# Unused matmuls, transposes and a value step moved in the opening; three second-layer groups first in each new chunk

## The chip, the cores and the metric

The kernel runs on one core of one Trainium2 chip. The core has five engines that run side by side and wait for each other through semaphores: the tensor engine (PE, with the loading of its weights shown apart as PEld), the vector engine (DVE), the scalar engine (ACT), the GpSimd engine (POOL) and the sync engine (SP). Transfers are issued from the queues of SP, ACT and POOL.

The metric is device time in microseconds (us). Before the change the median of 4 runs is 345.02 us (344.25 to 345.93). The execution that was profiled took 344.6 us, of which 342.9 us are the span from the first to the last instruction.

## The reference

Eight batches of eight-head causal attention over 576 tokens, with 16 "beacon" keys and values ahead that every query sees, then two dense layers with a leaky ReLU between:

```python
scores = scale * np.matmul(q, k_all.transpose(0, 1, 3, 2))   # q 8x8x576x64, k_all 8x8x592x64
scores = np.where(causal, -1000000000.0, scores)
...
a = np.exp(scores)
a /= a.sum(-1, keepdims=True) + 1e-09
attn_out = np.matmul(a, v_all)
...
x = attn_out.transpose(0, 2, 1, 3).reshape(4608, 512)
h = x @ w_in                    # 512 -> 2048
g = np.maximum(0.01 * h, h)
out = g @ w_out                 # 2048 -> 512
```

## The kernel before

**Attention.** The 64 heads are taken two at a time: a pair g (0 to 31, four to a batch) has one head in partitions 0 to 63 and the other in 64 to 127. For a pair the kernel turns q and k so that the head dimension lies on partitions, multiplies keys by queries into a score tile in PSUM, takes the exponential on ACT (line 262, or 310 for later pairs), clears what lies above the diagonal on POOL (line 275), multiplies by the values together with a column of ones (line 342, "value"), and divides on DVE (lines 351 and 352). The result x_nat is turned into xT, 512 features by 4608 tokens.

Pairs 0 to 7 (the opening, two batches) are turned on PE: `t_q` (line 217) issues 18 small transposes for q or k of a pair (line 229), and DVE or ACT copies the result out of PSUM (line 235). Pairs 8 to 31 are turned by DMA from SP (line 165), and so is their x_nat (lines 376 to 384).

**The dense layers.** Tokens are taken in nine chunks of 512. For a chunk, `up` (line 467) is one of 16 first-layer groups: four matmuls of 512 columns (line 395) and a leaky ReLU on ACT into gT (line 402). `down` (line 474) is one of 16 second-layer groups: four matmuls (line 433); four such groups make one 128-row output tile, which DVE copies to osb (line 445) and SP sends out (line 446). A chunk's second layer needs all of its first layer.

**Order.** The order of every engine's instructions is the order in which the program issues them. In the opening it is written out by hand as strings of steps: `q3` and `k3` are the transposes of pair 3 with their copies, `s2.1` is score tile 1 of pair 2 with its exponential, `m2.1` is a part of its masks on POOL, `v0.0` is the first half of the value product of pair 0, `l5.0` is a load of q (5.1: of k) for pair 5, `V` loads values, `i` and `o` load halves of the two weights, `x` turns a pair's x_nat on PE, `u` and `d` are one `up` and one `down`. `w6` is six unused matmuls of a zero matrix with 128 columns (line 480), and `W0.0.4` four of 112 columns that go into the PSUM buffer that `v0.0` will use (line 485). They compute nothing that is read.

From pair 8 on a list of events (lines 597 to 619) says at which point in the sequence of pairs loads, turns, score blocks, value steps and x turns are issued, and ahead of each event the program issues so many `up` and `down` groups through `fill` (line 456) that the rest is spread evenly. The plan keeps back KEPT = 3 groups for the moment when a new chunk of tokens becomes ready (`finish`, line 503, at the last pair of a batch). At that moment `finish` sets `turn` to 1, and `fill` then alternates: a `down`, an `up`, a `down`, and so on while second-layer groups are left.

```python
        if can1 and (turn[0] == 0 or not can2):
            up()
        elif can2:
            down()
```

The first `up` of a new chunk reads the xT that the last pair's x turn writes by DMA.

Of the kernel before, what the change touches and what calls it, by code (L numbers as in the profile page):

```python
# [15 lines left out]
def kernel(  # L16
# [93 lines left out]
    def make_ones():  # L110
        for t in v_bufs:
            nc.vector.memset(t[:, :, :, D : D + 1], 1.0)
# [30 lines left out]
    def load_qk(g, which):  # L143
        b, hp, grp, rows = where(g)
        loaded["qk", g, which] = nc.gpsimd.dma_start(  # L145
            out=raw_of(b, grp)[which][rows],
            in_=(q, k)[which][b, 2 * hp : 2 * hp + 2].rearrange("h (p i) d -> p h i d", i=RI),
        )
# [119 lines left out]
    def mask(g, part):  # L268
        aT = probs[g]
        for lo, n, rows in MASKS[part]:  # L270
            triangle(aT, lo, n, rows)
# [87 lines left out]
    def x_transposes(g, copy):  # L359
        b, hp = divmod(g, NPAIR)  # L360
        x_nat, _ = xs.pop(g)
        ps = ps_one.tile([128, 1024], BF16, name="tp", tag="one")
        for t, (q0, rows) in enumerate(QT):
            nc.tensor.transpose(
                ps[:, q0 : q0 + rows],
                x_nat[0:rows, t].rearrange("p e d -> p (e d)"),
                ident[0:rows, 0:rows],
            )
        copy(out=xT[:, hp, b * S : (b + 1) * S], in_=ps[:, 0:S])
# [81 lines left out]
        nc.scalar.copy(out=osb[:, n:], in_=acc[:, n:])  # L451
        nc.scalar.dma_start(out=out[t0 : t0 + 128, n:], in_=osb[:, n:])

    done1, done2, ready, turn, first_down = [0], [0], [0], [0], [0]

    def fill():
        i1, fc = divmod(done1[0], NF)
        i2, n2 = divmod(done2[0], NF)
        can1 = i1 < ready[0] and (i1 < 2 or i2 > i1 - 2)
        can2 = i2 < NCH and i2 < i1 and done1[0] >= first_down[0]  # L460
        if can1 and (turn[0] == 0 or not can2):
            up()
        elif can2:
            down()
        return can1 or can2

    def up():
        i1, fc = divmod(done1[0], NF)
        assert i1 < ready[0]
        moe1(i1, fc)  # L470
        done1[0] += 1
        turn[0] = 1

    def down():
        i2, n2 = divmod(done2[0], NF)
        moe2(i2, n2 // 4, n2 % 4)
        done2[0] += 1
        turn[0] = 0

    def unused(n, cols=128):  # L480
        ps = ps_one.tile([128, 512], FP32, name="av", tag="one")
        for i in range(n):
            nc.tensor.matmul(out=ps[:, 0:cols], lhsT=blank, rhs=blank[:, 0:cols], start=True, stop=True)  # L483
# [7 lines left out]
            )  # L491

    NG = B * NPAIR

    def has(g):
        return 0 <= g < NG

    dve, act, pool = nc.vector.tensor_copy, nc.scalar.copy, nc.gpsimd.tensor_copy

    def chunks_with(g):  # L500
        return (g + 1) // NPAIR * S // 512

    def finish(g, eng=0):
        if eng < 2 and g in xs:
            x_transposes(g, (dve, act)[eng])
        ready[0] = chunks_with(g)
        if g % NPAIR == NPAIR - 1:
            turn[0] = 1

    def run(steps):  # L510
        for step in steps.split():
            op, a = step[0], [int(x) for x in step[1:].split(".")] if step[1:] else []
            if op == "s":
                score(*a)
            elif op == "m":
                mask(*a)
            elif op == "v":
                value(*a)
            elif op == "x":
                finish(*a)  # L520
            elif op == "l":
                load_qk(*a)
            elif op == "V":
                load_v_cast(*a)
            elif op == "N":
                load_natural(*a)
            elif op == "T":
                turn_pair(a[0])
            elif op == "y":
                x_turn(a[0])  # L530
            elif op == "q" or op == "k":
                t_q(a[0], 0 if op == "q" else 1, (dve, act)[a[1] if len(a) > 1 else 0])
            elif op == "b":
                beacon_columns(a[0], (dve, act, pool)[a[1]])
            elif op == "u":
                up()
            elif op == "P":
                moe1_early(*a)
            elif op == "d":
                down()  # L540
            elif op == "w":
                unused(*a)
            elif op == "W":
                unused_ahead(*a)
            elif op == "i":
                load_w_in(a[0])
            elif op == "o":
                load_w_out(a[0])
            else:
                raise ValueError(step)  # L550
# [11 lines left out]
    with order:  # L562
        load_first_keys()
        load_beacon_k(0, 2, nc.scalar)
        nc.vector.memset(blank, 0.0)  # L565
        run("l0.0 l1.0")
        make_identity(nc, ident)
        make_ones()
        run("l1.1 l2.0 l2.1 V0.0 V0.1 V0.2 l3.0 l3.1 V0.3 V0.4 l4.0 l4.1 i0")
        make_pads()  # L570
        unused(24)
        cast_beacon_k(0, 2, nc.scalar.copy)
        beacon_transposes(0, 2)
        unused(10)
        nc.scalar.copy(out=k_nat0[:, :, 0], in_=first_k[:, 0])
        nc.vector.tensor_copy(out=k_nat0[:, :, 1], in_=first_k[:, 1])
        run("q0.1 k0 w6 s0.0 m0.0 q1 s0.1 k1 w6 s0.2 m0.1 w6 s0.3 m0.2")
        run("w6 s1.0 m1.0 q2 s1.1 k2 w6 s1.2 m1.1 w6 s1.3 m1.2 W0.0.4 s2.0 m2.0 W0.0.4 s2.1 v0.0 q3 l5.0 l5.1 s2.2 k3 m2.1 s2.3 i1 m2.2 W0.1.4 s3.0 m3.0 v1.0 s3.1 v0.1 s3.2 v1.1 m3.1 l6.0 l6.1 s3.3 x0.1 m3.2")
        run("v2.0 l7.0 l7.1 q4 v2.1 V1.0 V1.1 x1 k4.1 v3.0 v3.1 x2.1 s4.0 s4.1 x3 m4.0 V1.2 V1.3 V1.4 u s4.2 u s4.3 m4.1 m4.2 o0 u q5 k5 u")
        load_beacon_k(2, B, nc.gpsimd)  # L580
        run("s5.0 s5.1 m5.0 u u s5.2 s5.3 m5.1 m5.2 o1 u q6 k6 u v4.0 u v4.1 s6.0 s6.1 m6.0 u y4 N8.0 N8.1 u s6.2 s6.3 m6.1 m6.2 u")
        cast_beacon_k(2, B, nc.gpsimd.tensor_copy)
        run("q7 u k7 u v5.0 u v5.1 y5 N9.0 s7.0 s7.1 m7.0 d v6.0 v6.1 d y6 T8 s7.2 s7.3 m7.1 m7.2 N9.1 T9")
        beacon_transposes(2, B)
        run("b8.2 b9.2 b10.2 b11.2 u v7.0 v7.1 d d d d N10.0 N10.1 V2.0 V2.1 V2.2 V2.3 V2.4 d d N11.0 N11.1 x7")


        CUTS = [(0, 512, 1024, 1536, 1664), (0, 384, 896, 1376, 1664), (0, 224, 736, 1248, 1664)]
        BLOCKS = [((0, 0),), ((0, 1),)], [((0, 2),), ((0, 3), (1, 0))], [((1, 1),), ((1, 2),)], [((1, 3), (2, 0)), ((2, 1),)], [((2, 2),), ((2, 3),)]
        FIRST = 2 * NPAIR  # L590

        def block(g0, i):
            for tile in BLOCKS[i]:
                stretch([(g0 + r, CUTS[r][n], CUTS[r][n + 1]) for r, n in tile])

        events = []
        for g in range(FIRST, NG):
            if g > FIRST + 3:
                events.append((g - 3.6, 0, run, ("N%d.0" % g,)))
                events.append((g - 3.1, 0, run, ("N%d.1" % g,)))  # L600
            if g > FIRST + 1:
                events.append((g - 2.0, 0, run, ("T%d" % g,)))
            if g > FIRST + 3:
                events.append((g - 1.9, 0, run, ("b%d.2" % g,)))
            events.append((g + 2.25, 3, value, (g, 0)))
            events.append((g + 2.62, 4, value, (g, 1)))
            events.append((g + 2.63, 5, x_turn, (g,)))
            if (g - FIRST) % 3 == 0:
                for i in range(5):
                    events.append((g + (0.31 if g == FIRST else 0.01) + 0.6 * i, 2, block, (g, i)))  # L610
        ends = [FIRST]
        for g in range(FIRST, NG):
            events.append((g + 3.5, 2, finish, (g, 2)))
            if g % NPAIR == NPAIR - 1:
                ends.append(g + 3.5)
        for b in range(3, B):
            for n in range(NKB):
                events.append((4 * b - 0.9 + 0.3 * n, 6, load_v_cast, (b, n)))
        events.sort(key=lambda e: e[:2])
        KEPT = 3  # L620
        first_down[0] = 4
        w, d0 = 0, done1[0] + done2[0]
        for at, _, what, args in events:
            while w + 2 < len(ends) and at > ends[w + 1]:
                w, d0 = w + 1, done1[0] + done2[0]
            todo = 2 * NF * ready[0] - KEPT - d0
            aim = d0 + todo * (at - ends[w]) / (ends[w + 1] - ends[w])
            while done1[0] + done2[0] < aim and fill():
                pass
            what(*args)  # L630
        while done2[0] < NCH * NF:
            fill()
# [30 lines left out]
```

## Time and profile before

| what | us |
|---|---|
| median of 4 runs | 345.02 (344.25 to 345.93) |
| profiled execution | 344.6 |
| its span | 342.9 |
| ACT busy | 187.0 (55% of the span) |
| POOL busy | 181.1 (53%) |
| DVE busy | 81.6 (24%) |
| first-layer matmuls, 576 of 379 ns each on average | 139.0 |
| second-layer matmuls, 576 of 379 ns | 136.6 |
| value matmuls, 960 of 196 ns | 41.6 |
| score matmuls of pairs 8 to 31 | 24.4 |
| unused matmuls of 128 columns, 70 | 6.8 |

Matmuls are pipelined, so the duration of one matmul is longer than the distance from its start to the next one's; distances between starts are what a chain of them costs. A line of the timeline has the start, the time from first start to last end, the engine, the line of the kernel, what it writes and reads, the count, and in brackets the idle time ahead of it with what ended that. The profiler's clock row gives the share of the tensor engine's full clock that was granted.

### The profile page before, as it was taken

The page shows a single profiled execution, that of the slowest core. Times are in us where ns is not written, and L with a number is a line of the kernel's source. Part 1 is how long each engine was busy: PE and PEld are TensorE (multiplying, and loading weights), DVE is VectorE, ACT ScalarE, POOL GpSimd, SP SyncE. Part 2 cuts the span into 40 slices and gives each one's busy share as a digit, 9 for nine tenths or more (in the row PEclk, how much of TensorE's full clock was granted, in tenths as well). Part 3 has the DMA queues.
Part 4 walks back from the last instruction along what each step waited for, and adds up shares of the span by engine and source line. Part 5 has one row for each costly group of instructions (what it writes and reads, how often), then busy time and mean ns, then how long its engine had stood idle before and what let it go on. Part 6 is the DMA issues. An engine that isn't in the chain of part 4 may idle for free.

```text
span 342.9 us, 7415 instructions
## 1 busy us (share of the span) xinstructions
PE 333.1 (97%) x2978; PEld 168.6 (49%) x2978; DVE 81.6 (24%) x199; ACT 187.0 (55%) x280; POOL 181.1 (53%) x355
## 2 busy tenths in 40 slices
PE   8899999989998999999999999999999999999995
PEld 6574555435544454554454544554445544444442
DVE  4363343102322212221231123212321220000111
ACT  5868862668645784388347852775447205633300
POOL 8895878859998594488566965682211000000000
PEclk9989999999999999999999999999999999999999
DMA  9999999999999999999999999998211030000021
GB/s 140 132 204 178 142 194 152 186 126 169 157 159 175 169 140 120 142 125 135 131 153 112 137 125 132 132 135 97 81 54 45 19 109 32 0 31 32 31 92 61
DMA packets 154322, 40.16 MB, mean 117 GB/s; under 512 B 144384, under 2 KB 148608, under 8 KB 154288
## 3 DMA queue, kind: packets, MB, share of 16 engines
q0 software_dynamic: 100848, 18.54, 80.8%
q1 hardware_dynamic: 53024, 20.96, 33.3%
q8 instruction: 23, 0.38, 0.5%
q10 hardware_dynamic: 416, 0.20, 0.2%
q14 instruction: 11, 0.09, 0.1%
HBM read 37.22 MB, written 9.44 MB: 136 GB/s over the span
## 4 chain that ended last, share of the span: by engine, by line
PE 84%; DMA 8%; POOL 4%; DVE 1%; SPq 1%; issue 1%; ACT 0%; DVEq 0%; POOLq 0%
PE acc L395 35%; PE acc L433 32%; PE av L342 9%; PE sc L297 5%; DMA v_aug<-in_v_dram 5%; DMA xT<-x_nat 2%; DMA q_nat<-in_q_dram 2%; PE sc L253 2%; POOL v_aug L200 1%; POOL k_nat L157 1%; PE tp L229 1%; SPq L165 1%; POOL q_raw L145 0%; DVE qT L235 0%; POOL q_nat L157 0%
## 5 line engine op out<-in xcount | busy, mean ns | idle before, releaser
L395 PE MATMUL acc<-xT,w_in_sb 128*128 128x512 bf16 x576 | 139.0, 379 | 1.4 <-DMA xT<-x_nat 1.4
L433 PE MATMUL acc<-w_out_sb,gT 128*128 128x512 bf16 x576 | 136.6, 379 | 0.0
L402 ACT ACTIVATE gT<-acc 128x512 bf16<-128x512 f32 x144 | 85.2, 606 | 79.7 <-PE acc L395 79.0
L310 ACT ACTIVATE aT<-sc 128x1024 bf16<-128x1024 f32 (+3 forms) x96 | 76.8, 867 | 47.9 <-PE sc L297 46.3
L275 POOL TENSOR_SCALAR_AFFINE_SELECT aT<-aT 128x256 bf16<-128x256 bf16 (+2 forms) x160 | 57.6, 387 | 65.6 <-ACT aT L310 60.2
L433 PEld LDWEIGHTS <-gT 128*128 128x128 bf16 x576 | 53.7, 98 | 62.3 <-issue 2.5
L395 PEld LDWEIGHTS <-w_in_sb 128*128 128x128 bf16 x576 | 52.2, 98 | 60.5 <-issue 2.7
L445 DVE COPY osb<-acc 128x512 f32<-128x512 f32 x35 | 24.2, 691 | 92.1 <-PE acc L433 91.4
L351 DVE RECIPROCAL rec<-av 128x6 f32<-128x6 f32 (+1 forms) x64 | 12.0, 188 | 141.2 <-PE av L342 141.2
L342 PEld LDWEIGHTS <-aT 128*128 128x128 bf16 (+1 forms) x960 | 37.4, 99 | 15.2 <-issue 3.5
L342 PE MATMUL av<-v_aug,aT 128*128 128x65 bf16 (+1 forms) x960 | 41.6, 196 | 1.3 <-POOL aT L275 0.5
L157 POOL DMA_DIRECT2D k_nat<-in_k_dram x48 | 34.8, 731 | 4.0 <-DMA v_aug<-in_v_dram 3.0
L157 POOL DMA_DIRECT2D q_nat<-in_q_dram x48 | 34.8, 730 | 3.1 <-DMA v_aug<-in_v_dram 1.8
L200 POOL DMA_DIRECT2D v_aug<-in_v_dram x40 | 34.0, 857 | 3.2 <-DMA w_in_sb<-in_moe_w_in_dram 3.1
L352 DVE TENSOR_TENSOR x_nat<-av,rec 128x384 bf16<-128x384 f32 (+1 forms) x64 | 31.4, 490 | 2.2
L262 ACT ACTIVATE aT<-sc 128x1024 bf16<-128x1024 f32 (+3 forms) x32 | 26.5, 877 | 5.7 <-PE sc L253 5.6
L297 PE MATMUL sc<-qT,kT 64*128 64x208 bf16 (+16 forms) x368 | 24.4, 255 | 0.8 <-DMA kT<-k_nat 0.8
L297 PEld LDWEIGHTS <-kT 64*128 64x128 bf16 x368 | 12.3, 94 | 19.7 <-issue 17.9
L253 PE MATMUL sc<-qT,kT 64*128 64x80 bf16 (+4 forms) x96 | 10.4, 293 | 0.7 <-DVE kT L235 0.7
L235 DVE COPY qT<-tp 128x576 bf16<-128x576 bf16 x7 | 5.3, 754 | 13.3 <-PE tp L229 9.9
L483 PE MATMUL av<-blank 128*128 128x128 bf16 x70 | 6.8, 260 | 1.1 <-DVE blank L565 1.1
L451 ACT COPY osb<-acc 128x256 f32<-128x256 f32 x1 | 0.4, 372 | 13.7 <-DVE osb L449 13.7
(44 smaller groups left out, 67.4 us busy)
## 6 DMA issues: line engine op xcount, KB each, us to landing
out_dram<-osb SPq DMA_DIRECT2D x35, 256.0 KB, 2.6
q_nat<-in_q_dram POOLq DMA_DIRECT2D x48, 72.0 KB, 4.6
k_nat<-in_k_dram POOLq DMA_DIRECT2D x48, 72.0 KB, 4.7
v_aug<-in_v_dram POOLq DMA_DIRECT2D x24, 128.0 KB, 6.2
w_in_sb<-in_moe_w_in_dram POOLq DMA_DIRECT2D x2, 1024.0 KB, 12.0
w_out_sb<-in_moe_w_out_dram POOLq DMA_DIRECT2D x2, 1024.0 KB, 11.5
q_raw<-in_q_dram POOLq DMA_DIRECT2D x8, 144.0 KB, 8.1
k_raw<-in_k_dram POOLq DMA_DIRECT2D x7, 144.0 KB, 8.5
```

The costliest lines, as they stand in the source:

```text
L157: nc.gpsimd.dma_start(out=t[:, :, par], in_=(q, k)[which][b, 2 * hp + par].rearrange("(t p) d -> p t d", p=NR),)
L200: nc.gpsimd.dma_start(out=dst[lo : ROWS[c], c, :, 0:D], in_=v[b, :, OFF[c] : OFF[c] + n].rearrange("h p d -> p h d"),)
L262: nc.scalar.activation(out=aT[:, :, c0 : c0 + w], in_=sc[:, :, 0:w], func=AF.Exp, scale=0.125)
L275: nc.gpsimd.affine_select(out=view, in_=view, compare_op=ALU.is_ge, fill=0.0, base=128 - n if lo == 0 else 0, channel_multiplier=-1, patte ...
L297: nc.tensor.matmul(out=sc[:, par, at : at + b - a], lhsT=kT[ps_, c * 128 : (c + 1) * 128], rhs=qT[ps_, q0 : q0 + b - a], start=True, stop= ...
L310: nc.scalar.activation(out=probs[g][:, :, lo:hi], in_=sc[:, :, at : at + hi - lo], func=AF.Exp, scale=0.125)
L342: nc.tensor.matmul(out=avv[:, n, 0 : D + 1], lhsT=aT[0 : ROWS[c], par, a0 : a0 + 128], rhs=va[0 : ROWS[c], c, 2 * hp + par, :], start=(c = ...
L352: nc.vector.tensor_tensor(out=x_nat[:, t0:t1].rearrange("p t e d -> p (t e) d"), in0=avv[:, :, 0:D], in1=rec[:, n0:n1, None].to_broadcast( ...
L395: nc.tensor.matmul(out=acc, lhsT=w_in_sb[:, j, fc * 128 : (fc + 1) * 128], rhs=xT[:, j, i * 512 : (i + 1) * 512], start=(j == 0), stop=(j ...
L402: nc.scalar.activation(out=gT[i][:, fc, :], in_=acc, func=AF.Prelu, alpha=0.01)
L433: nc.tensor.matmul(out=acc, lhsT=gT[i][:, fc, t * 128 : (t + 1) * 128], rhs=w_out_sb[:, fc, :], start=(fc == 0), stop=(fc == NF - 1),)
L445: nc.vector.tensor_copy(out=osb, in_=acc)
```

## The change

1. The unused matmuls ahead of the beacon keys' transposes become 25 instead of 24, those behind them (ahead of pair 0's transposes) 13 instead of 10.
2. Pair 1's query transposes go behind score tile 0.1 instead of ahead of it, its key transposes behind tile 0.2 instead of 0.1; of the unused groups among pair 0's tiles, 6 + 6 become 5 + 4.
3. `v0.0` goes from ahead of `q3` to behind `k3`, and two more unused matmuls of 112 columns stand ahead of `s2.2`.
4. `q5` and `k5` go ahead: `q5` ahead of `s4.3`, `k5` ahead of an `up` and `o0`.
5. When a new chunk becomes ready, up to three second-layer groups are issued ahead of its first `up`, in place of the alternation from the first on.

```diff
-    done1, done2, ready, turn, first_down = [0], [0], [0], [0], [0]
+    done1, done2, ready, turn, first_down, held = [0], [0], [0], [0], [0], [0]
...
-        if can1 and (turn[0] == 0 or not can2):
+        if held[0] and can2:
+            held[0] -= 1
+            down()
+        elif can1 and (turn[0] == 0 or not can2):
             up()
...
+    KEPT = 3
...
         if g % NPAIR == NPAIR - 1:
             turn[0] = 1
+            held[0] = KEPT
...
-        unused(24)
+        unused(25)
         cast_beacon_k(0, 2, nc.scalar.copy)
         beacon_transposes(0, 2)
-        unused(10)
+        unused(13)
...
-        run("q0.1 k0 w6 s0.0 m0.0 q1 s0.1 k1 w6 s0.2 m0.1 w6 s0.3 m0.2")
-        run("... s2.0 m2.0 W0.0.4 s2.1 v0.0 q3 l5.0 l5.1 s2.2 k3 m2.1 s2.3 ...")
-        run("... u s4.2 u s4.3 m4.1 m4.2 o0 u q5 k5 u")
+        run("q0.1 k0 w6 s0.0 m0.0 w5 s0.1 q1 s0.2 m0.1 k1 w4 s0.3 m0.2")
+        run("... s2.0 m2.0 W0.0.4 s2.1 q3 l5.0 l5.1 W0.0.2 s2.2 k3 v0.0 m2.1 s2.3 ...")
+        run("... u s4.2 u q5 s4.3 m4.1 m4.2 k5 u o0 u")
...
-        KEPT = 3
```

In the strings "..." stands for steps that are the same in both. PE gets three matmuls more in all (4 + 2 added, 3 taken away). POOL's instructions keep their order.

More of the change, by code (lines that the diff above doesn't have):

```diff
@@ L570 @@
         make_pads()
-        unused(24)
+        unused(25)
         cast_beacon_k(0, 2, nc.scalar.copy)
         beacon_transposes(0, 2)
-        unused(10)
+        unused(13)
         nc.scalar.copy(out=k_nat0[:, :, 0], in_=first_k[:, 0])
         nc.vector.tensor_copy(out=k_nat0[:, :, 1], in_=first_k[:, 1])
-        run("q0.1 k0 w6 s0.0 m0.0 q1 s0.1 k1 w6 s0.2 m0.1 w6 s0.3 m0.2")
-        run("w6 s1.0 m1.0 q2 s1.1 k2 w6 s1.2 m1.1 w6 s1.3 m1.2 W0.0.4 s2.0 m2.0 W0.0.4 s2.1 v0.0 q3 l5.0 l5.1 s2.2 k3 m2.1 s2.3 i1 m2.2 W0.1.4 s3.0 m3.0 v1.0 s3.1 v0.1 s3.2 v1.1 m3.1 l6.0 l6.1 s3.3 x0.1 m3.2")
-        run("v2.0 l7.0 l7.1 q4 v2.1 V1.0 V1.1 x1 k4.1 v3.0 v3.1 x2.1 s4.0 s4.1 x3 m4.0 V1.2 V1.3 V1.4 u s4.2 u s4.3 m4.1 m4.2 o0 u q5 k5 u")
+        run("q0.1 k0 w6 s0.0 m0.0 w5 s0.1 q1 s0.2 m0.1 k1 w4 s0.3 m0.2")
+        run("w6 s1.0 m1.0 q2 s1.1 k2 w6 s1.2 m1.1 w6 s1.3 m1.2 W0.0.4 s2.0 m2.0 W0.0.4 s2.1 q3 l5.0 l5.1 W0.0.2 s2.2 k3 v0.0 m2.1 s2.3 i1 m2.2 W0.1.4 s3.0 m3.0 v1.0 s3.1 v0.1 s3.2 v1.1 m3.1 l6.0 l6.1 s3.3 x0.1 m3.2")
+        run("v2.0 l7.0 l7.1 q4 v2.1 V1.0 V1.1 x1 k4.1 v3.0 v3.1 x2.1 s4.0 s4.1 x3 m4.0 V1.2 V1.3 V1.4 u s4.2 u q5 s4.3 m4.1 m4.2 k5 u o0 u")
         load_beacon_k(2, B, nc.gpsimd)
```

## The prediction

> **What bounds the kernel now.** I read the page first, then the PE's list of waits, the granted clock by stage, and the timeline around each wait.
>
> ```profile
> PE 333.1 (97%) x2978; PEld 168.6 (49%) x2978; DVE 81.6 (24%) x199; ACT 187.0 (55%) x280; POOL 181.1 (53%) x355
> ```
>
> PE is busy for 97% of the span and no other engine for more than 55%. So PE sets the end, and this change hardly alters its work (three unused matmuls more). It can gain only idle time of PE and stretches in which PE ran at a lower clock. The list of PE's waits (us in total, times, longest) shows all idle time but the start and the end:
>
> ```profile
> PE acc L395 <- DMA xT<-x_nat: 1.4, 1, 1.4
> ...
> PE sc L297 <- DMA kT<-k_nat: 0.8, 1, 0.8
> PE sc L253 <- DVE kT L235: 0.7, 2, 0.4
> PE av L342 <- POOL aT L275: 0.5, 1, 0.5
> ```
>
> The clock, in a table by stage (stretch and its length; busy us and instructions of PE, PEld, DVE, ACT, POOL; granted clock; DMA). Column PEclk is the one to read:
>
> ```profile
> 11.57:14.99 3.42, 2.83 (x35) 1.52 (x32) 0.68 (x1) 3.42 (x5) 2.12 (x5) 1.00 2.95 127
> 14.99:18.40 3.41, 2.69 (x60) 1.75 (x61) 2.08 (x4) 1.83 (x3) 3.41 (x10) 1.00 1.65 150
> 18.40:21.81 3.41, 3.41 (x50) 2.50 (x49) 1.36 (x4) 2.46 (x3) 3.40 (x9) 0.50 1.13 208
> ```
>
> From 18.40 to 21.81 us PE ran at half clock, after a stretch in which it was busy 2.69 of 3.41 us. That loss is in no list of waits.
>
> **The change part by part.**
>
> *Extra unused matmuls (25 and 13).* The first group runs at 107 ns from start to start, so one more moves the beacon transposes from 3.74 to 3.85. The second group ran from 4.09 to 5.12 and PE then waited until 5.48 for pair 0's q, which landed at 5.4 (issued 1.33, 4.1 us to landing). Thirteen from 4.20 on (seven of about 107 ns, the rest at 56) have started by 5.2. Cost 0; if the clock rises later than at 4.75, all at 107 ns, they end near 5.6: 0.1 us.
>
> *Pair 1's transposes one tile later.* ACT works without a gap from 7.12 to 15.41 on the first ten score tiles. Now 0.1 starts at 7.3, ahead of ACT's need at 8.1; then q1 (0.40 us), 0.2 at 8.2 when its PSUM tile is free (8.56 before), k1 at 8.5; DVE has copied it by 9.7, ahead of 1.0 at 9.96. Cost 0 as long as that margin of 0.25 us lasts.
>
> *v0.0 behind k3.* This is the heart of the opening. Before:
>
> ```profile
> 13.76 0.37 PE L253 MATMUL sc<-qT,kT 64*128 64x464 bf16 x2
> 14.64 0.69 PE L342 MATMUL av<-v_aug,aT 128*128 128x65 bf16 x8 [0.51 <-POOL aT L275]
> 15.55 0.28 PE L342 MATMUL av<-v_aug,aT 128*128 128x65 bf16 x4 [0.23 <-DMA v_aug<-in_v_dram]
> 15.93 0.47 PE L229 MATMUL tp<-ident,q_raw 64*64 64x64 bf16 x18
> 16.33 0.35 PE L253 MATMUL sc<-qT,kT 64*128 64x336 bf16 x4
> 16.65 0.47 PE L229 MATMUL tp<-ident,k_raw 64*64 64x64 bf16 x18
> 17.05 0.30 PE L253 MATMUL sc<-qT,kT 64*128 64x208 bf16 x4
> 17.28 0.37 PE L489 MATMUL av<-blank 128*128 128x112 bf16 x4
> 18.05 0.39 PE L253 MATMUL sc<-qT,kT 64*128 64x512 bf16 x2 [0.39 <-DVE kT L235]
> ```
>
> It looks as if v0.0 held q3 up. But PEld shows that q3's first weight load also waited 0.22 us for its own data: pair 3's q was issued at 8.04 with 7.8 us to landing, so it is there at 15.84; its k (8.63 + 8.0) at 16.6. POOL's order is the same, so these landings stay. q3, now directly behind tile 2.1, stands idle from 14.1 to about 15.9, and behind it on PE wait tiles 2.2, 2.3, k3 and v0.0; ACT waits for 2.2 as before. Then: q3 15.93, two unused 16.33, tile 2.2 16.44 (16.33 before), k3 16.75, v0.0 17.15 (12 matmuls at 33 ns, 0.40), tile 2.3 17.55, four unused 17.8, tile 3.0 when DVE has copied k3. DVE takes q3 and k3 now without v0.0's division between, and ends at 17.98 (18.00 before). So tile 3.0 starts at 18.0 against 18.05: v0.0 fills the 0.39 us in which PE waited for that copy, and what was saved there is spent waiting at q3. v0.0's own division, now at 18.0, is needed only by x0. Bounds: were pair 3's data there in time, tile 2.2 would start near 14.7 and up to 1.3 us (ACT's gap there) would go; were the copies late, 0.4 lost. I take 0, by the landing.
>
> *The clock.* First the row: the loss of 18.40 to 21.81 is measured by the same chains at full clock elsewhere. There 12 value matmuls, a tile, 18, a tile, 18 took 0.78 + 0.50 + 1.10 + 0.46 + 0.92 = 3.76 us in the chain of waits; at full clock they take 0.37 + 0.30 + 0.66 + 0.28 + 0.66 = 2.27. Loss 1.5 us. The Trainium skill, "TensorE: Matmul & The Clock Gate" (HAM oscillation and the table behind it), asks only that PE have no idle gap over some 3 us; by that rule neither kernel would ever fall to half clock here and fillers are worth 0. The trace disagrees: the longest gap in the stretch was 0.51 us. [...]I sum, over each of the two stretches, columns streamed (0.44 us per 1000 columns, from 56 ns for 128, pairs on separate rows once): 50% from 11.57 to 14.99, no fall after it; 47% from 14.99, fall. With the new order I get some 47% and 52%: the first now has half of the idle time. (The page calls these stretches free-running; where they lie in other executions this trace does not show.) The same page's Part 4 says that transposes do not count as other matmuls do; without q3 and k3 the two become 47% and 38%, against 50% kept and 33% lost before. By the one count the fall may come at 15.0, by the other at 15.0 or 18.4; hardly any count removes it. Falling at 15.0 it would stretch q3 to tile 3.0: two transposes +0.2 each, tiles +0.3, v0.0 +0.3, unused +0.15, about 1.2 us for the 1.5. Bounds: -1.5 (no fall) to +1.2 (both). I take 0.
>
> *q5 and k5 earlier.* Tile 5.0 waited 0.34 us at 32.5 for k5's copy, with one `up` between. Now two `up` (1.7 us) stand between k5 and tile 5.0 and DVE is idle from 27.6: the wait goes, -0.34. q5's data landed at 26.3 and 27.0. o0's issue on POOL does not move.
>
> *Three second-layer groups first.* Timeline of the new chunk that waited:
>
> ```profile
> 106.44 0.81 PE L395 MATMUL acc<-xT,w_in_sb 128*128 128x512 bf16 x3
> 108.68 0.39 PE L395 MATMUL acc<-xT,w_in_sb 128*128 128x512 bf16 x1 [1.43 <-DMA xT<-x_nat]
> ```
>
> Three matmuls of `up` ran, the fourth waited 1.43 us for pair 11's xT: SP issued its last turn at 101.91 and it landed 6.7 us later. In the order of the new kernel two more `down` stand ahead of this `up`, 2 x 0.865 = 1.73 us; the fourth matmul would come at 107.25 + 1.73 = 108.98, after the landing at 108.64. The wait goes: -1.43. At the other chunks nothing waited. On SP the output's issue now precedes a pair of turns (pair 17's, 111.03): it waits for `down` and its copy, up to 0.55 us for turns issued two pairs ahead. ACT gets its leaky ReLUs in a row, 0.6 us each behind 0.87 of PE. Cost 0.
>
> The kT wait at 74 us (0.8) hangs on loads that POOL issues after its masks at 52.7, which wait for ACT; it moves with PE and stays.
>
> **Sum:** 344.6 - 0.34 - 1.43 = 342.8 for the profiled execution. That one lies 0.42 below the median, so the median becomes 345.02 - 1.77 = about 343.2.
>
> **The rivals.**
>
> *A, the clock does not fall* (or pair 3's data come earlier): 343.2 - 1.4 = 341.8; more is not to be had, as the first weight half lands at 25.5 (13.4 + 12.1) and the first `up` at 26.96 needs it. For: by plain columns no stretch lies far below what was kept. Against: the idle 1.8 us in one piece.
>
> *B, the gain is small*: the xT transfer took 6.7 us where the median turn takes 4.4; in executions where it lands by 107.2, nothing waits and nothing goes. With a later clock window on work now packed, +0.5, only 344.5 to 345.2 is left. For: the wait occurs once. Against: SP issued without a gap for 8 us ahead of it, so it is no accident.
>
> *C, slower: SP.* At six chunks an output, which waits for PE, is put ahead of two turns on SP's queue. From 91 to 111 SP issues almost back to back at 1.2 us each. If turns fall behind until scores wait as they did at 74 us (0.83), six chunks cost 5.0, less 1.77: 348.2. It decides once the delay passes the lead of about two pairs (18 us), so I think it unlikely; with a fall of the clock twice and no gain at xT (+0.9) the slower side has more.
>
> That the change does not do what it says is excluded: the instruction order shows the moves.
>
> **How the numbers follow.** No change can be told within 0.5% (1.7 us), so 343.3 and 346.7 are the limits. Main case 50% (its own range 342.3 to 344.2, half of it on each side of 343.3), A 20%, B 16%, C and the doubled fall of the clock 14%. Faster 0.25 + 0.20 with a little for gains in both, 0.48; slower 0.14; the rest, 0.38, is within. The range takes in A below and B and the single surplus fall above: 341.3 to 346.0.
>
> **What would show it.** In the profile after: no wait of L395 for xT near 107 us; no wait of L253 near 32; q3 starting at 15.9 with 1.8 us of idle PE ahead of it, named as q_raw; tile 3.0 near 18.0; one stretch of 3.4 us at half clock, from 15.0 or 18.4. A q3 at 14.2, no half clock, or SP's turns late for scores would each prove a step wrong.

## The result, and the profile after

The changed kernel takes 342.75 us (median of 43 runs, 340.31 to 348.86), the kernel before 345.52 (64 runs, 342.66 to 352.42). The ratio, which leaves out executions more than 1.5% above the fastest of their kernel, is 0.9919 with a 95% interval of 0.9903 to 0.9935: 2.2 to 3.4 us less. The forecast was 343.2 us, 1.8 less than the median then known. The time lies within the stated range, but the gain is larger than the forecast's sum, and what makes up the difference stays open below.

The profiled execution of the changed kernel took 342.69 us, its span 341.0 (before 344.6 and 342.9). First the list of PE's waits after the change, complete (us in total, times, longest):

```profile
PE tp L229 <- DMA q_raw<-in_q_dram: 1.5, 1, 1.5
PE av L486 <- DVE blank L570: 1.1, 1, 1.1
PE acc L395 <- DMA xT<-x_nat: 0.5, 1, 0.5
```

The wait for xT fell from 1.4 to 0.5, both waits of line 253 for DVE's copies are gone, and so is that for kT. One long wait at q3 stands where several short ones stood. The timeline of PE there (start, time, engine, line, what, count, idle time ahead) shows it:

```profile
13.63 0.37 PE L253 MATMUL sc<-qT,kT 64*128 64x464 bf16 x2
15.49 0.69 PE L229 MATMUL tp<-ident,q_raw 64*64 64x64 bf16 x18 [1.50 <-DMA q_raw<-in_q_dram]
16.12 0.37 PE L492 MATMUL av<-blank 128*128 128x112 bf16 x2
16.42 0.53 PE L253 MATMUL sc<-qT,kT 64*128 64x336 bf16 x4
16.88 0.69 PE L229 MATMUL tp<-ident,k_raw 64*64 64x64 bf16 x18
17.50 0.84 PE L342 MATMUL av<-v_aug,aT 128*128 128x65 bf16 x12
18.27 0.42 PE L253 MATMUL sc<-qT,kT 64*128 64x208 bf16 x4
18.62 0.56 PE L492 MATMUL av<-blank 128*128 128x112 bf16 x4
19.11 0.60 PE L253 MATMUL sc<-qT,kT 64*128 64x512 bf16 x2
```

Tile 3.0 starts at 19.11, not at 18.0: from 15.29 to 22.12 everything runs at half clock, as the table by stage says (length; busy us and count of PE, PEld, DVE, ACT, POOL; clock; DMA):

```profile
11.88:15.29 3.41, 2.12 (x26) 1.12 (x22) 0.24 (x1) 3.41 (x5) 1.75 (x5) 1.00 2.55 138
15.29:18.71 3.42, 3.21 (x60) 2.27 (x61) 1.82 (x4) 0.86 (x1) 3.42 (x11) 0.50 1.36 171
18.71:22.12 3.41, 3.41 (x40) 2.23 (x42) 1.21 (x3) 2.62 (x3) 3.31 (x9) 0.50 1.11 206
```

After a stretch with PE busy for only 2.12 of 3.41 us the clock was halved for two stretches instead of one. So the opening of this execution was slower: its first `up` started at 27.84 us, in the profile before at 26.96. And yet the end came 1.9 us earlier. The new chunk near 107 us, in PE's timeline:

```profile
105.50 1.89 PE L433 MATMUL acc<-w_out_sb,gT 128*128 128x512 bf16 x8
107.23 0.81 PE L395 MATMUL acc<-xT,w_in_sb 128*128 128x512 bf16 x3
108.49 2.12 PE L395 MATMUL acc<-xT,w_in_sb 128*128 128x512 bf16 x9 [0.45 <-DMA xT<-x_nat]
```

Eight more second-layer matmuls (two groups) now run ahead of the `up`. PE came to this `up` at 107.23, not at the 106.44 + 1.73 = 108.17 of the forecast's sum, because it was already early before the chunk; so the landing at 108.45 still holds the fourth matmul for 0.45 us.

Two theories then. **Lead theory:** part 5 alone brings the gain, and transfers that PE meets at 73 to 75 and at 108 us take up what the opening gains or loses. **Sum theory:** the parts add up, the opening's share with them.

### The profile page after: what moved, and what is told of

It reads as the page before. It is cut to its first block, busy times and chain, and to the rows that moved or that the text cites. A ratio compares the mean times of both kernels' runs of the same rounds, so it can differ in the third digit from the quotient of the medians.

```text
span 341.0 us, 7421 instructions
## 1 busy us (share of the span) xinstructions
PE 333.8 (98%) x2981; PEld 169.4 (50%) x2981; DVE 81.9 (24%) x199; ACT 186.7 (55%) x280; POOL 181.1 (53%) x355
## 4 chain that ended last, share of the span: by engine, by line
PE 78%; POOL 9%; DMA 9%; issue 2%; SPq 1%; DVE 0%; ACT 0%; POOLq 0%
PE acc L395 33%; PE acc L433 29%; PE av L342 8%; PE sc L297 4%; DMA v_aug<-in_v_dram 3%; DMA q_raw<-in_q_dram 2%; DMA xT<-x_nat 2%; POOL v_aug L200 2%; POOL aT L275 2%; POOL k_nat L157 2%; DMA k_nat<-in_k_dram 2%; PE sc L253 2%; POOL q_nat L157 1%; PE tp L229 1%; POOL q_raw L145 0%
## 5 line engine op out<-in xcount | busy, mean ns | idle before, releaser
L395 PE MATMUL acc<-xT,w_in_sb 128*128 128x512 bf16 x576 | 136.9, 379 | 0.5 <-DMA xT<-x_nat 0.5
```

What stands on the lines that cost most here:

```text
L395: nc.tensor.matmul(out=acc, lhsT=w_in_sb[:, j, fc * 128 : (fc + 1) * 128], rhs=xT[:, j, i * 512 : (i + 1) * 512], start=(j == 0), stop=(j ...
```

## The experiments

Each was timed beside the kernel before on the same chip. A ratio of 0.9935 is 2.2 us less. The "changed kernel" is the one above.

**Part 5 alone**, put into the kernel before:

```diff
-        if can1 and (turn[0] == 0 or not can2):
+        if held[0] and can2:
+            held[0] -= 1
+            down()
+        elif can1 and (turn[0] == 0 or not can2):
...
+            held[0] = KEPT
```

> The kernel before with part 5 alone (three second-layer groups first in each new chunk). Lead theory: the transfers at 73 to 75 us and at 108 us take up whatever the opening gains or loses, so this part alone brings nearly all of the change: 2.0 to 2.8 us less than before, and little or no wait of L395 for xT near 107 us. Sum theory: the parts add up, so this one brings only the 1.4 us of that wait, and the rest belongs to the opening.

Measured: 342.95 us, ratio 0.9935 (0.9902 to 0.9968). There is no wait for xT in its profile. It has the opening of before, with its waits, and by the ratios it still has four fifths of the gain. Its interval (1.1 to 3.4 us less) holds the expectations of both theories.

**Part 5 alone, again**, together with the changed kernel again, on one chip.

> Part 5 alone once more. Lead theory: within 0.4 us of the changed kernel of the same call. If the opening's gains come through once the wait at 108 us is covered: 0.4 to 1.0 us slower than the changed kernel.

> The changed kernel once more, beside the run of part 5 alone on the same chip. Ratio 0.990 to 0.994. Its profile, with another fall of the clock, should show the waits at 38 and 73 to 75 us that the opening's gain is lost in, if the opening is early.

Measured: part 5 alone 343.51 us, ratio 0.9923 (0.9894 to 0.9952); the changed kernel 343.94 us, ratio 0.9939 (0.9900 to 0.9978). The intervals overlap almost wholly. Part 5 alone stands 0.4 us ahead by the medians and 0.6 by the ratios, where the rival expectation had it 0.4 to 1.0 behind. This speaks for the lead theory; that the opening adds something on top is not shown. In the new profile of part 5 alone, PE's timeline at the new chunk:

```profile
105.93 1.67 PE L433 MATMUL acc<-w_out_sb,gT 128*128 128x512 bf16 x7
107.44 2.75 PE L395 MATMUL acc<-xT,w_in_sb 128*128 128x512 bf16 x12
```

Twelve first-layer matmuls follow the second-layer ones without a gap. The waits that were expected of the changed kernel near 38 and 73 us were seen here (1.0 us at 37 and 0.6 at 73), but not in the changed kernel's second profile, which lost 1.3 us for kT at 62 us.

**The opening alone**, the changed kernel without part 5:

```diff
-            held[0] = KEPT
+            held[0] = 0
```

> The changed kernel without part 5 (held set to 0). Lead theory: no gain, within 0.4 us of before, because PE then waits the longer for xT near 107 us (1.4 us or more). Sum theory: 0.4 to 1.4 us less than before, the wait for xT at 1.4 us or below and the tile of pair 5 near 32 us without a wait.

Measured: 344.93 us, ratio 1.0010 (0.9978 to 1.0042): no gain is seen. PE's list of waits for it:

```profile
PE acc L395 <- DMA xT<-x_nat: 1.5, 1, 1.5
PE tp L229 <- DMA q_raw<-in_q_dram: 1.1, 2, 0.6
PE av L342 <- DMA v_aug<-in_v_dram: 1.1, 1, 1.1
...
PE sc L297 <- DMA kT<-k_nat: 1.0, 1, 1.0
```

The wait of tile 5.0 for DVE's copy is gone, as forecast, but a wait for values (at 38.6 us) and one for kT (74.8) stand behind it, and xT is as late as before. This is against the sum theory, though of its 0.4 to 1.4 us the interval still allows up to 0.8.

**Part 3 undone** in the changed kernel:

```diff
- s2.1 q3 l5.0 l5.1 W0.0.2 s2.2 k3 v0.0 m2.1
+ s2.1 v0.0 q3 l5.0 l5.1 s2.2 k3 m2.1
```

> The changed kernel with part 3 undone: v0.0 ahead of q3 again, without the two unused matmuls. Lead theory and my prediction's reading of part 3 (worth nothing, q3 waits for its own data): within 0.4 us of the changed kernel; tile 3.0 starts within 0.3 us of where it starts in the changed kernel when both have the same clock. If part 3 is what gained beyond the forecast: 0.8 to 1.3 us slower than the changed kernel.

Measured: 343.14 us, ratio 0.9942 (0.9914 to 0.9969), 0.8 us above the changed kernel by the ratios, with intervals that overlap widely. That settles neither the 0.4 us of the first expectation nor the 0.8 of the rival. In its profile v0.0 waited 2.19 us for masks, and the clock was halved from 17.72 to 24.55. Its first `up` came at 28.89 us, the latest in the table below, and its span is still only 341.8 us.

**Pair 3's loads ahead.**

```diff
- V0.0 V0.1 V0.2 l3.0 l3.1 V0.3
+ V0.0 V0.1 l3.0 l3.1 V0.2 V0.3
```

> The changed kernel with the loads of pair 3's q and k issued ahead of the third value load. If q3 waits for its own data alone, that wait (1.5 us in the profile) goes and q3 starts near 14.2; v0.0 then waits for the third value load, near 16.6. Lead theory: the first up comes earlier, by up to 1 us, and the time stays within 0.4 us of the changed kernel, because the transfers at 73 us take it up. Sum theory: 0.5 to 1.2 us less than the changed kernel.

Measured: 343.10 us, ratio 0.9934 (0.9900 to 0.9968): no better. q3 now starts at 14.12 without a wait, so it did wait for its own data; the first `up` came at 25.08. Where that lead went is in PE's timeline:

```profile
35.69 0.25 PE L342 MATMUL av<-v_aug,aT 128*128 128x65 bf16 x3
36.39 0.32 PE L342 MATMUL av<-v_aug,aT 128*128 128x65 bf16 x5 [0.44 <-DMA v_aug<-in_v_dram]
37.82 0.30 PE L342 MATMUL av<-v_aug,aT 128*128 128x65 bf16 x4 [1.12 <-DMA v_aug<-in_v_dram]
```

v4.0, in three pieces, waited 1.6 us in all for its values. After the stretch with these waits the clock was halved, later than in any other profile; the table by stage says:

```profile
34.54:37.95 3.41, 1.82 (x27) 0.89 (x22) 1.33 (x2) 1.49 (x3) 3.40 (x8) 1.00 2.79 91
37.95:41.36 3.41, 3.41 (x30) 1.72 (x27) 1.22 (x4) 0.60 (x1) 1.77 (x4) 0.50 1.15 165
```

These runs make one table. "First up" is the start of the first first-layer group, "value 8" the start of the last of the 12 matmuls of pair 8's first value step, "last" the start of PE's last matmul, all in us of each profile:

| kernel | first up | value 8 | last | last less value 8 |
|---|---|---|---|---|
| before | 26.96 | 75.41 | 338.52 | 263.11 |
| opening alone | 26.45 | 75.53 | 338.88 | 263.35 |
| changed | 27.84 | 74.45 | 336.61 | 262.16 |
| changed, again | 26.53 | 74.26 | 335.77 | 261.51 |
| part 5 alone | 27.34 | 75.54 | 337.13 | 261.59 |
| part 5 alone, again | 24.93 | 74.67 | 336.18 | 261.51 |
| part 3 undone | 28.89 | 75.76 | 337.46 | 261.70 |
| pair 3's loads ahead | 25.08 | 75.53 | 337.03 | 261.50 |

First ups spread over 4.0 us; at value 8 the spread is 1.5 us, and the two ends (28.89 and 24.93) lie 1.1 apart. Behind value 8 the kernels fall into two groups: 263.1 to 263.4 without part 5, 261.5 to 261.7 with it, and 262.2 where 0.45 us of the wait was left. Part 5 is worth 1.6 us there. The wait's line says 1.43, but that counts from the modelled end of the matmul ahead of it. By starts, the fourth matmul of that `up` came 1.81 us behind the third in the profile before, where the usual distance is 0.22: the wait cost 1.59 us.

**The idle time ahead of q3 filled.**

```diff
- s2.1 q3
+ s2.1 W0.0.24 q3
```

> The changed kernel with 24 unused matmuls of 112 columns in the idle time ahead of q3 (1.2 us at full clock). If idle time there is what halves the clock: no half clock between 12 and 23 us, and the first up near 26.5 instead of 27.8. Lead theory: the time all the same within 0.4 us of the changed kernel. If the clock in the opening counts for the end: 0.5 to 1.5 us less.

Measured: 342.70 us, ratio 0.9945 (0.9912 to 0.9978). The first `up` came at 25.94; the median is that of the changed kernel, and by the ratios nothing is gained. In the list of PE's waits:

```profile
PE av L342 <- POOL aT L275: 1.1, 1, 1.1
...
PE tp L229 <- DMA q_raw<-in_q_dram: 0.4, 1, 0.4
```

The value step that waits 1.1 us stands at 38.4 us; the wait is put down to POOL, whose masks for it stand behind two DMA issues. The clock was full from its first rise until PE had ended:

```profile
4.68:339.18 334.50, 326.46 (x2929) 165.76 (x2971) 80.66 (x186) 184.83 (x278) 177.49 (x345) 1.00 1.10 118
339.18:340.24 1.06, 0.00 (x0) 0.00 (x0) 0.00 (x0) 0.00 (x0) 0.00 (x0) 0.50 0.00 0
```

The mean granted clock of this execution is 0.998, and the missing part is the half clock of the second row, when PE had no work left. One stretch of 3.41 us at half clock would make 0.995. So of the 12 timed executions only one (0.995) has such a stretch; eleven stand at 0.997 or above. Of all executions of the three kernels with this filling (two follow below) 28 of 33 do, of the changed kernel's 31 of 56. The filling keeps the clock up in most executions, and yet no gain of time shows.

**Pairs 8 to 10 later.**

```diff
-                    events.append((g + (0.31 if g == FIRST else 0.01) + 0.6 * i, 2, block, (g, i)))
+                    events.append((g + (0.48 if g == FIRST else 0.01) + 0.6 * i, 2, block, (g, i)))
...
-            events.append((g + 2.25, 3, value, (g, 0)))
+            events.append((g + 2.25 + 0.17 * (g == FIRST), 3, value, (g, 0)))
```

> The changed kernel with the score tiles of pairs 8 to 10 and the first value step of pair 8 issued 0.17 of a pair (1.5 us of fill work) later. If PE's waits at 73 to 75 us are what takes up the opening's gains: they go, and the time falls by 0.3 to 1.0 us below the changed kernel, unless the wait for xT near 107 us grows by as much. If the transfers only stall PE at a later place: within 0.3 us of the changed kernel, with the new place in the list of waits.

Measured: 343.03 us, ratio 0.9942 (0.9906 to 0.9978). No wait at 73 to 75 us is left, and no time is gained. A value step waited 0.9 us for POOL's masks at 37 us instead, and a score tile 0.4 us for ACT at 80 us.

**Five groups instead of three.**

```diff
-    KEPT = 3
+    KEPT = 5
```

> The changed kernel with KEPT = 5: five second-layer groups kept for each new chunk and issued first. The wait for xT that is left near 108 us (0.5 us in the changed kernel's profile) goes. Lead theory: 0.2 to 0.6 us less than the changed kernel. If three groups already cover the landing in most executions: the same within 0.3 us.

Measured: 343.72 us, ratio 0.9971 (0.9938 to 1.0004), 1.0 us worse than the changed kernel by the medians and 1.8 by the ratios, against both expectations. Groups that are kept for the new chunk are missing as filling before it, so PE comes to the attention work of a batch earlier. In the profile:

```profile
73.06 0.49 PE L297 MATMUL sc<-qT,kT 64*128 64x224 bf16 x6 [1.14 <-POOL aT L275]
73.48 1.04 PE L395 MATMUL acc<-xT,w_in_sb 128*128 128x512 bf16 x4
```

This tile waited 1.14 us (another, at 84 us, 0.63). In the terms of the table, "last less value 8" is 262.31, 0.6 to 0.8 above the kernels of the table with part 5 and no wait for xT: about the wait at 84 us.

**Both of these together.**

> Both: pairs 8 to 10 later by 0.17 of a pair, and KEPT = 5. If the waits at 73 to 75 and at 108 us are in series and each hides what is gained ahead of it, only both together let the opening's gain through: 0.8 to 1.5 us less than the changed kernel. If transfers stall PE elsewhere: no less than the better of the two alone.

Measured: 344.00 us, ratio 0.9971 (0.9944 to 0.9999): the cost of the five groups stays (0.86 us of waiting at 85 us; last less value 8 is 262.40, against 261.38 with pairs 8 to 10 later alone), and no gain comes through.

**v4.0 later** in the kernel with the filled wait, **and all together.**

```diff
- k6 u v4.0 u v4.1
+ k6 u u v4.0 v4.1
```

> The changed kernel with the 24 unused matmuls ahead of q3 and with v4.0 issued one first-layer group later, since v4.0 waits near 38 us for its values (1.1 us) whenever the opening is early. If that wait takes up the opening's gain: it goes, and the time falls 0.4 to 0.9 us below the changed kernel. If the wait only moves to 73 us: within 0.3 us of the changed kernel.

Measured: 344.62 us, ratio 0.9934 (0.9896 to 0.9973). Its profiled execution took 346.68 us and cannot show the effect of the step: there PE ran at half clock from the start until 20.73 us, where the other profiles show the first rise at 3.8 to 6.5, and the first `up` came at 31.10. With pairs 8 to 10 later as well:

> As the run before, and pairs 8 to 10 later by 0.17 of a pair too, so that neither the wait at 38 nor that at 73 us is met. If these are the last places that take up the opening's gain: 0.6 to 1.2 us less than the changed kernel. If transfers end by what they carry and PE meets them later: within 0.3 us of it.

Measured: 342.65 us, ratio 0.9912 (0.9876 to 0.9948). The waits at 38 and at 73 us are gone from its profile, but its first `up` is at 26.51 and one group behind it waited 0.8 us. The lowest ratio here, but its interval holds the changed kernel's. No version is shown to beat it.

## Why the prediction was right, point by point

**Three groups first (forecast -1.43): right in kind, a little low.** The wait goes, wholly in five of the six profiles with three groups in the table, down to 0.45 in one. Behind value 8 it is worth 1.6 us, which is the 1.59 that the wait cost by starts: the forecast took the idle time from a modelled end, which left out 0.16. The two groups last 1.73 us, and that is the most they can cover. Part 5 alone measured 1.1 to 3.4 and 1.7 to 3.7 us.

**q5 and k5 earlier (forecast -0.34): the wait goes, the gain does not come.** The opening alone has no wait at tile 5.0 and no gain that the interval shows. The step that failed is the sum: I added the 0.34 as if nothing later waited for transfers. In the opening alone PE then waits 1.0 us for kT at 74.8 and 1.5 for xT at 109.

**v0.0 behind k3 (forecast 0): the mechanism is right, the size is not settled.** q3 stood idle until its own data landed, named as such (it started at 15.49, forecast 15.9); with the loads ahead it started at 14.1. Undoing the part left the time 0.8 us higher by the ratios, with intervals that overlap. Tile 3.0 came at 19.11 instead of 18.0, because the clock was halved from 15.29 on, one of the two places given.

**The clock (forecast 0, bounds -1.5 to +1.2).** In the profile it was near the upper bound: two stretches instead of one, first `up` 0.88 us later. The reading behind the forecast was wrong in one place: the gap of 0.51 us ended at 14.64 and lies in the stretch that kept the clock, while the longest gap in the stretch ahead of the fall was 0.39.

What a stretch costs at the end can be read from the timed executions that the ratios use, several chips together, by their mean granted clock. At 0.997 or more, with no stretch at half clock while PE worked, the changed kernel has a median of 342.2 us (24 runs), before 344.4 (37); with about one stretch 342.8 (14) and 345.5 (27); with two or more 343.4 (6) and 346.2 (25). So a stretch goes with 0.6 to 1.1 us, less than the 1.5 us worked out for PE alone, and in each class the change brings 2.3 to 2.8. The mean leaves out the time ahead of the clock's first rise, so that differences in this rise stay inside the classes.

**kT's wait at 74 us ("stays"): wrong for the profile, right as a place.** It is absent in the profile after, where PE came to it late, and there at 73 to 75 us in three others of the table, 0.3 to 1.0 us. That it moves with PE was the error: the loads ahead of it move far less than PE does. Pair 8's last value load landed at 73.8 (before), 72.9 (changed), 74.2 (part 3 undone) and 73.9 us (loads ahead), while the first ups of these lie 3.8 us apart; for all eight kernels of the table the landings lie within 1.6 us.

**Extra unused matmuls and pair 1's transposes (0):** q0's transposes start at 5.42 (5.48 before), the first exponential at 7.06 (7.12) and tile 1.0 at 9.83 (9.96): nothing lost.

**The rivals.** SP's order cost nothing: behind 75 us no score tile waits for a turn in either profile of the changed kernel. "The clock does not fall" would have been 341.8; the executions of the highest class above have 342.2, and the opening's gain there is not shown. The reason given for a limit there was wrong too: the first `up` can start before 26.96, and did so at 24.93 (part 5 alone, again) and 25.08 (loads ahead). The small gain of rival B is excluded by the interval.

Between the 1.6 us behind value 8 and the 2.2 to 3.4 of the timed runs 0.6 to 1.8 us are left. In the profiles this rest lies ahead of value 8, where two profiles of one kernel differ by up to 0.9 us (part 5 alone, twice). Whether the opening gives a part of it is open: by the ratios the changed kernel stands ahead of part 5 alone where they were timed apart (0.9919 and 0.9935) and behind it where they were timed together (0.9939 and 0.9923). So the forecast had the main cause right, with nearly its size. That its sum came within half a microsecond of the median is in part luck: the 0.34 in it did not come, and the rest, which is larger, was not in it.

## What to carry to other kernels

Independent work that has been kept back belongs ahead of the first instruction that reads a late transfer, together and not in alternation; its worth is the smaller of the length moved ahead and the wait. Here 1.73 us moved ahead of a wait that cost 1.59 brought 1.6. What is kept back is missing earlier: five groups cost more than they covered. When waits for transfers stand in series, a gain ahead of them can be lost in them (first ups 4.0 us apart became 1.5 at value 8), so do not add it to a gain behind them unless the profile shows that it arrives.

## What the runs showed of the hardware

In seven profiles the clock was halved while PE worked. Each of these falls came three, four or ten times 3.41 us behind the clock's first rise, and lasted 3.41 or 6.83 us. None followed an idle gap near 3.41 us: the longest in the stretch ahead of a fall was 2.19 us (part 3 undone), in the profile before 0.39.

Is it then the share of work in a stretch, as the forecast took it to be? As an estimate I count the columns streamed, with 0.42 us for 1000 at full clock (0.216 us from start to start for 512) and pairs on separate rows once. The stretches ahead of a fall have shares of about 0.23 to 0.43. Stretches with 0.42 (part 5 alone, the filled wait) and 0.44 (pairs 8 to 10 later with five groups) passed without a fall, so this count is no sharp threshold. Without the transposes it sorts worse: 0.15 to 0.36 ahead of a fall, and 0.28 to 0.35 in several that passed. So no run here shows that transposes count less.

Once halved, a stretch filled to about 0.74 (changed) or 0.76 (part 3 undone) did not bring the clock back; in all seven profiles it came back after a stretch filled to 0.80 or more. I had counted on one stretch ending by itself.
